# Feature attention into a PReLU MLP on one core: the last three token tiles on a permuted copy of x, other store shapes, fillers in the head, and a new order of all work

## The chip, the core and the metric

The kernel runs on one core of one Trainium2 chip. The core has TensorE (PE, matrix products, its weight loads shown apart as PEld), VectorE (DVE), ScalarE (ACT), GpSimd (POOL) and SyncE (SP, which here only issues transfers), each with its own queue worked through in order, and 16 DMA engines between the chip's memory (HBM) and the on-chip SBUF. PE writes into PSUM, eight banks of 128 partitions by 512 float32. The metric is the device time of one execution in microseconds (us), as the median of several runs; lower is better.

## The reference

An attention without softmax: queries and keys become 64 features each (the products of two 8-wide sketches), and every head's output is a ratio of two sums over these features. The heads' outputs, 4 x 1088 tokens of 4 x 32 = 128 columns, are the input x of an MLP with a hidden width of 2048 and a leaky relu whose slope `alpha` differs by column.

```python
def phi(x):                       # S1, S2: 8 x 32
    a = np.einsum('rd,bhsd->bhsr', S1, x)
    b = np.einsum('rd,bhsd->bhsr', S2, x)
    return np.einsum('bhsi,bhsj->bhsij', a, b).reshape(*x.shape[:-1], r * r)
q_p, k_p = (phi(q), phi(k))       # q, k, v: 4 batches, 4 heads, 1088, 32
kv = np.einsum('bhsf,bhsd->bhfd', k_p, v)
z = np.sum(k_p, axis=2)
num = np.einsum('bhsf,bhfd->bhsd', q_p, kv)
den = np.einsum('bhsf,bhf->bhs', q_p, z)[..., None] + 1e-06
x = (num / den).transpose(0, 2, 1, 3).reshape(4352, 128)
h = x @ w_in                      # 128 x 2048
g = np.maximum(h, 0.0) + alpha * np.minimum(h, 0.0)
out = g @ w_out                   # 2048 x 128
```

## The kernel before

**The MLP.** The leaky relu is split as alpha * h + (1 - alpha) * relu(h). The linear part is one 128 x 128 matrix W = w_in diag(alpha) w_out, made once (`Wmm`, copied by `W`). So the output is x W + relu(x w_in) w_a, with w_a = (1 - alpha) w_out. x lies in SBUF as `x_sb`, one column for each token and 128 partitions for the heads' columns. A batch has 34 groups of 32 tokens that came from 128-partition loads in which partition p holds tokens 34p to 34p + 33; so the columns are not in token order.

**The tiles.** `mlp` (L618) is called for ten tiles: tiles 0 to 6 have 512 tokens (two of each batch but the last), tile 7 ("the rest tile") takes the last 64 columns of all four batches, 256 tokens, and tiles 8 and 9 have 256 tokens each of the last batch. In a tile, `h` steps (L632) multiply x with 128 columns of w_in into a bank, `r` steps (L643 on ACT, L645 on DVE) apply relu and write bfloat16 into one of ten buffers `rh`, `o` steps (L653, L655) multiply with w_a and add up in the tile's output bank, and a `W` step adds x W. A name such as r8.12 is tile 8, hidden chunks from 12 on; in tiles 7 to 9 a step covers two chunks, with four 128-column matmuls in an `o` step (L653). Tiles 0 to 6 come out with output columns on partitions; DVE transposes them (`oT`, L683) and four stores go out per tile (L695). Tiles 7 to 9 take x or relu as the stationary operand and come out with tokens on partitions: two copies (`oT7.0`, `oT7.1`, L690) and a store of rows (L708, `store_rows`, two stores for tile 9, one on SP and one on ACT). For that, their relus write a permuted layout (L640), and their W step is eight matmuls of 32 columns of x each (L663).

**The attention.** For each batch, keys are transposed on DVE (`k1T0`), multiplied by the sketch (`k1f0`, L480), transposed back (`k1fT0`), multiplied elementwise (`k1p0`, mostly on POOL), summed (`zs10`, L504, and `z`/`zS`/`C`) and multiplied with v (`kv10`, L515, then `kvc`, `fin`, `kvR`). Queries run alike (`q1T0`, `q1f`, `q1t`, `q1rc`, `q1b`, `q1p0`, `q1p1`, `q1PT0`, `q1PT1`, `q1n` on PE at L547, and `q1x0`, `q1x1`, which write x). The first 512 queries of batch 0 take a shorter way: `qaT0` and `qaT1` (L563), `qaa0` to `qab1` (L571), `qac`, `qam`, the denominators `den0` and `den1` (L580) with `zcB`, the reciprocals `rc0` and `rc1` (L589), the numerators `num0` and `num1` (L594), and `xA0` and `xA1` (L596). The head is bound by these steps while k, q, v and the weights arrive.

**The order.** Nothing is scheduled at run time. A string `ORDER` (L22) names every step once, with its engine (p, a, d, g for POOL, s) and the numbers of the buffers it takes (PSUM banks and SBUF slots); `arrange` (L93) issues the steps in that order, and each engine has its steps in its queue in that order. A number behind the p is a count of filler matmuls issued ahead of the step (`dummy`, L274), products of constants whose result nobody reads; `warm` is 34 such units at the start.

Of the kernel before, what the change touches and what calls it, by code (L numbers as in the profile page):

```python
# [34 lines left out]
w_hi2:a r1.7:a:7 Wmm0:p:2 Wmm1:p kv10:p:6 r1.6:a:0 k2T0:d:0 q1rc:d:1 r1.5:a:8 r1.4:a:9 q1b:d k2f0:p:4 w_lo2:d Wmm2:p Wmm3:p h1.8:p:3 r1.2:a:3
h1.9:p:7 k3T0:d:1 k2fT0:d:0 kvc1:a:1 fin1:p W:d k3f0:p:4 zs20:p:2 r1.9:a:2 h1.10:p:7 r1.10:a:5 r1.3:d:4 W1:p:0 o1.0:p q1p0:g:0 q1PT0:d:1 o1.1:p
o1.2:p k3fT0:d:1 r1.8:a:6 h1.11:p:7 q1p1:g q1PT1:d o1.3:p o1.4:p o1.5:p h1.12:p:4 o1.6:p W0:p oT0:d:0 o1.7:p z12:a:0 k3p1:g:2 o1.8:p r1.12:a:1 zS2:p
C2:d kvR1:a q1n:p:3 q2T0:d:2 r1.11:a:3 q1x0:a q1x1:d h1.13:p:1 h1.14:p:2 r1.14:a:4 r1.13:a:9 o1.9:p h1.15:p:7 o1.10:p ld_v3_2:s st0.0:s st0.1:s
st0.2:s st0.3:s h2.0:p:3 h2.1:p:4 o1.11:p r2.0:a:8 o1.12:p r1.15:d:0 r2.1:d:7 h2.2:p:5 h2.3:p:6 r2.2:a:6 o1.13:p h2.4:p:2 h2.5:p:7 h2.6:p:1 r2.3:a:2
o1.14:p o1.15:p oT1:d:1 q2f:p:3 q2fT:d:0 r2.5:a:5 W2:p:7 o2.0:p o2.1:p o2.2:p o2.3:p h2.7:p:0 r2.7:d:3 r2.4:a:1 o2.4:p h2.8:p:2 k3p0:g h2.9:p:3  # L40
h2.10:p:4 h2.11:p:5 r2.9:d:9 r2.8:d:4 o2.5:p k2p1:g:1 r2.6:a:0 r2.11:a:8 h2.12:p:1 h2.13:p:6 h2.14:p:0 o2.6:p o2.7:p r2.10:d:7 r2.13:a:6 h2.15:p:3
h3.0:p:5 r2.14:d:2 h3.1:p:2 r2.12:a:1 r3.0:a:5 q2t:g:0 q2rc:d:0 r3.1:d:0 q2b:d q2p1:d:0 h3.2:p:6 h3.3:p:4 o2.8:p o2.9:p h3.4:p:1 h3.5:p:0 h3.6:p:5
r2.15:a:3 r3.4:a:4 o2.10:p o2.11:p o2.12:p r3.2:a:9 r3.6:a:7 h3.7:p:3 r3.7:a:8 h3.8:p:2 h3.9:p:1 o2.13:p ld_v2:s o2.14:p r3.5:a:1 ld_q3:s h3.10:p:6
o2.15:p oT2:d:2 r3.9:a:6 k2p0:g r3.3:a:2 W3:p:5 o3.0:p r3.10:a:3 zs30:p:3 z13:d:1 q2p0:g ld_v2_1:s ld_v2_2:s st1.0:s st1.1:s st1.2:s st1.3:s ld_v3:s
ld_v2_3:s st2.0:s st2.1:s st2.2:s st2.3:s r3.8:a:5 kv20:p:0 kvc2:a:0 o3.1:p h3.11:p:1 q2PT0:d:0 zS3:p C3:d fin2:p q2PT1:d kvR2:a h3.12:p:7 h3.13:p:4
h3.14:p:6 o3.2:p r3.11:a:0 o3.3:p r3.14:a:9 q3T0:d:0 o3.4:p o3.5:p r3.12:a:2 o3.6:p q2n:p:0 h3.15:p:6 q2x1:a r3.13:d:4 o3.7:p o3.8:p o3.9:p o3.10:p
# [12 lines left out]
st6.3:s h8.2:p:2 W7:p:3 r7.0:a:4 h8.4:p:1 r8.0:a:1 h8.6:p:7 o7.0:p h8.8:p:0 h8.10:p:5 r8.2:d:8 o7.2:p r8.6:a:3 o7.4:p o7.6:p h8.12:p:2 r7.10:a:4
# [53 lines left out]
def kernel(  # L113
# [39 lines left out]
    def ps(b):  # L153
        return PS[:, b.slot] if b.n == 1 else PS[:, b.slot:b.slot + b.n]
# [614 lines left out]
```

## Time and profile before

| | us |
|---|---|
| median of 3 runs | 109.92 (109.7 to 110.33) |
| the profiled execution, its own time | 110.14 |
| its span, from first to last instruction | 108.0 |
| PE busy / DVE busy / ACT busy / POOL busy | 96.0 / 80.6 / 64.9 / 46.0 |
| last matmul ends | 100.2 |
| mean granted TensorE clock | 0.959 |

The profile's page gives busy times, the span in 40 slices and the chain of work that ended last; answers of the trace give stretches (busy time of each engine, granted clock and DMA share between two moments), the timeline, waits, and the DMA issues with the time to landing. Some 2.1 us of an execution lie outside its span. PE's busy time counts pipelined matmuls from start to end, so that a row may be longer than the distance to the next one: 0.22 us from one 512-column product to the next, while one lasts 0.38.

### The profile page before, as it was taken

What the parts mean: (1) busy time and instruction counts of PE and PEld (TensorE: products, weight loads), DVE (VectorE), ACT (ScalarE), POOL (GpSimd) and SP (SyncE); (2) the same over time, 40 slices, a digit from 0 to 9 for tenths busy, and PEclk for the clock granted to TensorE, in tenths of its full rate; (3) what the DMA queues carried; (4) which work ended last, traced back from release to release, by engine and by line L of the source; (5) the groups of instructions that cost most, each with busy time, mean ns of one, the idle gap of its engine ahead of it and who ended that gap; (6) DMA issues with size and microseconds to landing.
All of it is one profiled execution on the core that took longest, in us unless ns stands there. A gap on an engine that the chain in (4) does not pass through costs nothing.

```text
span 108.0 us, 3355 instructions
## 1 busy us (share of the span) xinstructions
PE 96.0 (89%) x1402; PEld 54.3 (50%) x1402; DVE 80.6 (75%) x134; ACT 64.9 (60%) x139; POOL 46.0 (43%) x48
## 2 busy tenths in 40 slices
PE   7859888898999999999999999999999999999100
PEld 2414544686567545344464455444444466989000
DVE  4764799999899999589959847899598968545100
ACT  2302349999999265947997455685447666765000
POOL 4619306999998989709390004960000000000000
PEclk9985999999999999999999999999999999999955
DMA  3999999999200004784204100320310041510110
GB/s 84 324 250 336 367 273 294 289 297 225 71 3 9 6 0 72 217 230 77 72 14 71 19 6 0 60 37 6 67 30 0 0 76 27 97 48 6 52 40 8
DMA packets 21462, 11.24 MB, mean 104 GB/s; under 512 B 15416, under 2 KB 19912, under 8 KB 21448
## 3 DMA queue, kind: packets, MB, share of 16 engines
q1 hardware_dynamic: 21270, 10.95, 39.6%
q8 instruction: 11, 0.18, 0.7%
q10 hardware_dynamic: 178, 0.08, 0.3%
q14 instruction: 3, 0.02, 0.1%
HBM read 8.80 MB, written 2.23 MB: 102 GB/s over the span
## 4 chain that ended last, share of the span: by engine, by line
PE 77%; DVE 6%; DMA 5%; POOL 3%; ACT 1%; SPq 1%; issue 1%; DVEq 0%
PE ps L632 25%; PE ps L655 23%; PE ps L547 5%; PE ps L653 5%; DMA q<-in_q_dram 5%; PE ps L515 4%; PE ps L571 3%; POOL P__73 L187 2%; PE ps L439 2%; PE ps L480 2%; PE ps L379 2%; DVE rr__101 L589 2%; PE ps L398 1%; PE ps L504 1%; PE ps L580 1%; POOL w_a_bf L187 1%
## 5 line engine op out<-in xcount | busy, mean ns | idle before, releaser
L632 PE MATMUL ps<-x,w_in_bf 128*128 128x512 bf16 (+1 forms) x176 | 38.9, 331 | 0.5 <-DVE x L596 0.3
L632 PEld LDWEIGHTS <-w_in_bf 128*128 128x128 bf16 x176 | 16.5, 98 | 13.6 <-issue 2.0
L655 PEld LDWEIGHTS <-w_a_bf 128*128 128x128 bf16 x128 | 12.2, 98 | 11.5 <-POOL w_a_bf L187 0.6
L643 ACT ACTIVATE rh__87<-ps 128x512 bf16<-128x512 f32 x10 | 6.1, 605 | 4.9 <-PE ps L632 2.9
L643 ACT ACTIVATE rh__83<-ps 128x512 bf16<-128x512 f32 x12 | 7.4, 618 | 2.0 <-PE ps L632 2.0
L643 ACT ACTIVATE rh__91<-ps 128x512 bf16<-128x512 f32 (+1 forms) x12 | 7.1, 591 | 0.8 <-PE ps L655 0.8
L643 ACT ACTIVATE rh__90<-ps 128x512 bf16<-128x512 f32 x9 | 5.5, 615 | 3.3 <-PE ps L632 3.1
L643 ACT ACTIVATE rh__85<-ps 128x512 bf16<-128x512 f32 x10 | 6.2, 619 | 2.1 <-PE ps L632 2.1
L187 POOL TENSOR_TENSOR P__72<-Fk__70 128x1024 f32<-128x1024 f32 (+1 forms) x2 | 4.3, 2167 | 5.3 <-DVE Fk__70 L485 5.3
L643 ACT ACTIVATE rh__84<-ps 128x512 bf16<-128x512 f32 x8 | 4.9, 616 | 1.7 <-PE ps L632 1.7
L180 ACT CAST x<-ps 128x576 bf16<-128x576 f32 (+1 forms) x5 | 2.9, 597 | 4.8 <-PE ps L547 4.7
L645 DVE TENSOR_SCALAR rh__82<-ps 128x512 bf16<-128x512 f32 x7 | 4.8, 679 | 1.3 <-PE ps L632 1.2
L643 ACT ACTIVATE rh__88<-ps 128x512 bf16<-128x512 f32 x9 | 5.5, 609 | 0.3 <-PE ps L632 0.2
L187 POOL TENSOR_TENSOR P__71<-Fk__69 128x512 f32<-128x512 f32 (+1 forms) x4 | 4.1, 1062 | 3.0 <-DVE Wf L182 3.0
L187 POOL TENSOR_TENSOR t__77<-F__68 128x288 f32<-128x288 f32 x2 | 1.6, 784 | 8.7 <-DVE F__68 L442 8.7
L643 ACT ACTIVATE rh__82<-ps 128x512 bf16<-128x512 f32 x8 | 4.9, 608 | 0.3 <-PE ps L632 0.3
L643 ACT ACTIVATE rh__86<-ps 128x512 bf16<-128x512 f32 x8 | 4.9, 606 | 0.4 <-PE ps L632 0.2
L655 PE MATMUL ps<-rh__83,w_a_bf 128*128 128x512 bf16 (+1 forms) x15 | 4.9, 351 | 0.0
L571 PE MATMUL ps<-qTa,Sab 32*64 32x256 f32 x32 | 3.8, 585 | 1.3 <-DVE qTa L563 1.3
L187 POOL TENSOR_TENSOR P__71<-F__68 128x1152 f32<-128x1152 f32 x2 | 4.6, 2336 | 0.5 <-DVE F__68 L187 0.5
L645 DVE TENSOR_SCALAR rh__86<-ps 128x512 bf16<-128x512 f32 x7 | 4.7, 670 | 0.2 <-PE ps L632 0.2
L645 DVE TENSOR_SCALAR rh__89<-ps 128x512 bf16<-128x512 f32 x6 | 4.1, 683 | 0.7 <-PE ps L632 0.6
(201 smaller groups left out, 236.9 us busy)
## 6 DMA issues: line engine op xcount, KB each, us to landing
v<-in_v_dram SPq DMA_DIRECT2D x12, 144.0 KB, 5.0
k<-in_k_dram SPq DMA_DIRECT2D x3, 544.0 KB, 9.2
q<-in_q_dram SPq DMA_DIRECT2D x3, 544.0 KB, 7.6
w_in_f<-in_moe_w_in_dram SPq DMA_DIRECT2D x2, 512.0 KB, 7.5
w_out_f<-in_moe_w_out_dram SPq DMA_DIRECT2D x4, 256.0 KB, 8.3
out_dram<-oT__92 SPq DMA_DIRECT2D x9, 64.0 KB, 1.8
out_dram<-oT__93 SPq DMA_DIRECT2D x8, 64.0 KB, 1.9
out_dram<-oT__95 SPq DMA_DIRECT2D x8, 64.0 KB, 1.9
```

The costliest lines, as they stand in the source:

```text
L180: nc.scalar.copy(dst, src)
L187: (nc.vector if e == "dve" else nc.gpsimd).tensor_tensor(out=dst, in0=a, in1=b, op=what)
L379: nc.tensor.matmul(ps(bw)[:, :DM], winT[:, c], w_hl[:, c, y], start=c == y == 0, stop=c == NC - 1 and y == 1)
L439: nc.tensor.matmul(ps(bf)[32 * g:32 * g + 32, h, :n], Wf[32 * h:32 * h + 32, b], src[1]()[32 * h:32 * h + 32, g * n:(g + 1) * n], start=Tr ...
L515: nc.tensor.matmul(ps(bk)[32 * h:32 * h + 32, :R], v_sb[b][:, h, j], bview(sb(P), [[1, R]], (4 * j + h) * R), start=j == 0, stop=j == JG - ...
L547: nc.tensor.matmul(ps(bn)[32 * h:32 * h + 32, g, :n], kvR[b][32 * g:32 * g + 32, y, 32 * h:32 * h + 32], bview(sb(Q)[32 * g:32 * g + 32], ...
L571: nc.tensor.matmul(ps(bp)[64 * (h % 2):64 * (h % 2) + 64, h // 2, 256 * y:256 * y + 256], bview(Sab[32 * h:32 * h + 32, y], [[1, R]]), qTa ...
L632: nc.tensor.matmul(ps(b)[:, n * i:n * i + n], w_in_bf[:, c], x(), start=True, stop=True, skip_group_check=len(cs) > 1)
L643: nc.scalar.activation(dst, src, ACTF.Relu)
L645: nc.vector.tensor_scalar_max(dst, src, 0.0)
L653: nc.tensor.matmul(ps(bo)[:, j // JB, DM * (j % JB):DM * (j % JB) + DM], rhs(j), w, start=False, stop=end, skip_group_check=True)
L655: nc.tensor.matmul(ps(bo)[:, lo:lo + n], w, rhs, start=first and lo == 0, stop=end, skip_group_check=True)
```

## The change

- Tiles 7 to 9 read x from a new buffer `xp` (three pieces of 256 columns). A step `xp0`, `xp1` or `xp2` copies each tile's columns from `x_sb` in another order, in which four columns of one partition of the loads lie side by side. `xp0` and `xp1` run on DVE, `xp2` on POOL.
- With it the relus of these tiles read and write straight, their W step is two matmuls of 128 columns, and partition 4a + b of the output holds row b of group a. The store of a tile goes out as one transfer whose outermost index has 32 values, with 4 rows of 1 KB inside; tile 9's second store, on ACT, is gone.
- `alT` (the transposed alpha) comes at the start of PE's work, with two fillers ahead, and `qaa1` has three fillers ahead.
- The cost of one load (`rate` of qa) that the planner of the order used is another; it has no effect at run time.
- `ORDER` is new throughout: order, engines and buffers.

```diff
-ld_k0.0:s wz:g ident:g pads9:g ld_rows:a zero:d ld_rows_1:a ld_k0.1:s selP:d M8i:d ld_qa:s warm:p M4:d ld_v0:s M8b:d identb:g E8:d M64:d ld_v0_1:s
...
+ident:g M8b:d M4:d ld_rows:a ld_k0.0:s pads:g ld_rows_1:a ld_k0.1:s ld_alpha:a warm:p alT:p2:0 zero:d table:a alTc:a selP:g M2:d k0T0:d:0 k0T1:d
...
     def mlp(g, halves, store, wfirst, xw=None, final=False):
-        bo = Buf("ps", 2 if xw else 1)
-        J = halves[0][0] // 128
-        JB = J // 2
+        bo = Buf("ps", 1 if xw is None else 2)
...
-                def re(e, b=b, br=br, w=w, nu=len(cs)):
-                    src, dst = ps(b)[:, :w], sb(br)[:, :w]
-                    if xw:
-                        src, dst = (bview(t, ap) for t, ap in ((ps(b), [[32 * J, 4 * nu], [32, J], [1, 32]]),
-                                                               (sb(br), [[32, 4 * nu], [128 * nu, J], [1, 32]])))
+                def re(e, b=b, br=br, w=w):
                     if e == "act":
-                        nc.scalar.activation(dst, src, ACTF.Relu)
+                        nc.scalar.activation(sb(br)[:, :w], ps(b)[:, :w], ACTF.Relu)
...
         def put(e, c, rhs, lo, n, w, first, end):
-            if xw:
-                for j in range(J):
-                    nc.tensor.matmul(ps(bo)[:, j // JB, DM * (j % JB):DM * (j % JB) + DM], rhs(j), w, start=False, stop=end, skip_group_check=True)
+            if xw is not None:
+                for j in range(2):
+                    nc.tensor.matmul(ps(bo)[:, j, :DM], rhs[:, 128 * j:128 * j + 128], w, start=first, stop=end, skip_group_check=True)
...
         def wp(e):
-            if xw:
-                for j in range(J):
-                    for i in range(4):
-                        nc.tensor.matmul(ps(bo)[32 * i:32 * i + 32, j // JB, DM * (j % JB):DM * (j % JB) + DM], xw(J * i + j), W_bf,
-                                         start=j % JB == 0, stop=False, skip_group_check=True)
-                return
...
-    def store_rows(off, outer, parts=(("sp", 4),)):
-        def st(g, os, boT, rows_of, J):
-            lo = 0
-            for i, (en, k) in enumerate(parts):
-                op({en: 600}, lambda e, lo=lo, k=k: (nc.scalar if e == "act" else nc.sync).dma_start(
-                    bass.AP(tensor=out.tensor, offset=off + lo * outer, ap=[[outer, k], [NJ * DM, 32], [1, J * DM]]),
-                    rows_of()[32 * lo:32 * lo + 32 * k, :J * DM]), os, [boT], name=f"st{g}.{i}", nbytes=16384 * J * k, rate=300.)
-                lo += k
+    def store_rows(off, step):
+        def st(g, os, boT, rows_of):
+            op({"sp": 600}, lambda e: nc.sync.dma_start(bass.AP(tensor=out.tensor, offset=off, ap=[[NJ * DM, 32], [step, 4], [1, 2 * DM]]),
+                                                        rows_of()[:, :2 * DM]), os, [boT], name=f"st{g}.0", nbytes=131072, rate=300.)
         return st
+
+    def paired(t, off, step, needs):
+        o = op({"pool": 600, "dve": V(256, "sb"), "act": A(256, "sb")}, lambda e: copy(
+            e, bview(xp[:, t], [[128, 2], [4, 32], [1, 4]]), bview(x_sb, [[32, 2], [1, 32], [step, 4]], off)), needs, name=f"xp{t}", port=True)
+        return [(256, lambda: xp[:, t], [o])]
...
-    mlp(g + 3, [(256, cols(B - 1, 768, 256), xs[B - 1])], store_rows(row0 + 24 * DM, 2 * DM, (("sp", 2), ("act", 2))), True, tile_of(B - 1, 768), True)
+    mlp(g + 3, paired(2, col0 + 768, 64, xs[B - 1]), store_rows(row0 + 24 * DM, 2 * DM), True, 2, True)
```

Three places of the new order, word for word as the instructions stand in the engines' queues.

SP's last rows before: `oT__95` holds tile 6's output here, `oT__94`, `oT__93` and `oT__92` those of tiles 7, 8 and 9 (behind the buffer stands the shape of the transfer).

```order
L695 DMA out_dram<-oT__95 32x16x32 x4
L708 DMA out_dram<-oT__94 128x256
L708 DMA out_dram<-oT__93 4x32x256
L708 DMA out_dram<-oT__92 2x32x256
L764 UNCONDITIONAL_BRANCH
```

SP's last rows in the changed kernel, tile 6 and then tiles 7 to 9:

```order
L682 DMA out_dram<-oT__92 32x16x32 x4
L693 DMA out_dram<-oT__93 32x4x256
L693 DMA out_dram<-oT__95 32x4x256
L693 DMA out_dram<-oT__92 32x4x256
L749 UNCONDITIONAL_BRANCH
```

The outermost count of tiles 7, 8 and 9 was 128 (its two outer dimensions are one), 4, and 2 on SP with 2 on ACT; now it is 32 for all three, and ACT has no store.

ACT in tiles 7 to 9 before, from r8.14 to r9.2 (the `rh` names are the relus' output buffers, `oT2__94` is tile 7's output):

```order
L643 ACTIVATE rh7__89<-ps_63 128x8x2x32
L643 ACTIVATE rh9__91<-ps_63 128x8x2x32
L180 COPY oT2__94<-ps_63 128x128
L643 ACTIVATE rh2__84<-ps_63 128x8x2x32
L180 COPY oT2__94<-ps_63 128x128
L643 ACTIVATE rh6__88<-ps_63 128x8x2x32
```

ACT in the changed kernel, r8.6, r8.8, r8.4, r8.0, r8.12, r8.10 and r9.2:

```order
L637 ACTIVATE rh1__83<-ps_63 128x512
L637 ACTIVATE rh7__89<-ps_63 128x512
L637 ACTIVATE rh9__91<-ps_63 128x512
L637 ACTIVATE rh4__86<-ps_63 128x512
L637 ACTIVATE rh2__84<-ps_63 128x512
L637 ACTIVATE rh5__87<-ps_63 128x512
L637 ACTIVATE rh0__82<-ps_63 128x512
```

Tile 7's two output copies have moved from ACT to DVE, and seven relus stand one behind the other on ACT.

PE in the head before, from the first products of k on (`Fk__69` holds the sketched keys of batch 0, `qTa` the first 512 queries):

```order
L480 MATMUL ps<-T__64,Wk 32x288 x8
L571 MATMUL ps<-qTa,Sab 64x256 x4
L504 MATMUL ps<-Fk__69 32x32 x4
L571 MATMUL ps<-qTa,Sab 64x256 x8
L504 MATMUL ps<-Fk__69 32x32 x5
L571 MATMUL ps<-qTa,Sab 64x256 x4
```

PE in the changed kernel, from the last of the three fillers behind the products of k on:

```order
L276 LDWEIGHTS const-bfloat16-1.0
L276 MATMUL ps<-const-bfloat16-1.0 128x128
L571 MATMUL ps<-qTa,Sab 64x256 x8
L504 MATMUL ps<-Fk__69 32x32 x9
L571 MATMUL ps<-qTa,Sab 64x256 x8
L421 MATMUL ps<-zA,E_124 128x32
```

The z sums (L504) have come together between the two halves of the query products (L571), of which the second 256 queries now come first.

109 lines of the change are left out of this document (53 added, 56 removed).

## The prediction

> **What bounds the kernel now.** I read the page first (span, busy shares), then its chain that ended last by engine, and then the busy time by stretches (each row: from, to, length, then each engine's busy time, the granted clock, the DMA share and GB/s).
>
> ```profile
> span 108.0 us, 3355 instructions
> PE 96.0 (89%) x1402; PEld 54.3 (50%) x1402; DVE 80.6 (75%) x134; ACT 64.9 (60%) x139; POOL 46.0 (43%) x48
> PE 77%; DVE 6%; DMA 5%; POOL 3%; ACT 1%; SPq 1%; issue 1%; DVEq 0%
> core 0: us, PE busy (x) PEld busy (x) DVE busy (x) ACT busy (x) POOL busy (x), PEclk, DMA share, GB/s
> 3.65:7.07 3.42, 2.04 (x24) 0.91 (x22) 2.31 (x7) 0.00 (x0) 0.98 (x4) 1.00 1.05 272
> 7.07:10.48 3.41, 3.25 (x35) 1.32 (x35) 2.19 (x6) 0.58 (x1) 2.83 (x3) 0.50 1.00 313
> 13.90:30.00 16.10, 14.71 (x309) 9.85 (x308) 15.34 (x26) 14.78 (x40) 12.66 (x10) 1.00 0.90 235
> 30.00:100.20 70.20, 70.18 (x967) 39.38 (x965) 56.37 (x84) 46.62 (x93) 26.33 (x16) 1.00 0.23 48
> ```
>
> Three stages with three limits. From 30.0 to 100.2 PE is busy 70.18 of 70.20 us at full clock: no order of the same matmuls can make this stage shorter, only fewer matmuls can, and a worse order can make it longer. Before 30 PE idles and once runs at half clock (7.07 to 10.48); DVE, busy 15.34 of 16.10 us, sets the pace there. Behind 100.2 nothing computes, and yet 7.8 us of the span are left. From the timeline, the chain, SP's waits, the stretches and the DMA issues (last number: us from issue to landing):
>
> ```profile
> 100.16 0.29 DVE L182 COPY oT__92<-ps 128x128 f32<-128x128 f32 x1 [0.53 <-PE ps L653]
> 100.20 0.02 issue
> 100.54 0.54 SPq L708 DMA_DIRECT2D out_dram<-oT__92  x1
> 100.54 0.64 ACTq L708 DMA_DIRECT2D out_dram<-oT__92  x1
> SPq L764 <- DMA out_dram<-oT__92: 5.1, 2, 3.8
> 96.50:97.50 1.00, 1.00 (x19) 0.79 (x16) 0.08 (x1) 0.67 (x2) 0.00 (x0) 1.00 0.37 131
> 101.00:102.50 1.50, 0.00 (x0) 0.00 (x0) 0.00 (x0) 0.00 (x0) 0.00 (x0) 1.00 0.25 82
> 103.00:104.50 1.50, 0.00 (x0) 0.00 (x0) 0.00 (x0) 0.00 (x0) 0.00 (x0) 0.50 0.13 37
> out_dram<-oT__94 SPq DMA_DIRECT2D x1, 128.0 KB, 1.7
> out_dram<-oT__94 SPq DMA_DIRECT2D x4, 64.0 KB, 3.3
> ```
>
> SP issues the last store at 100.54, is done with that at 101.08, and then waits 5.1 us for the two halves of tile 9's output: 106.2. The remaining 1.8 us to 108.0 are the closing waits and the barrier. While those stores run, the DMA share is 0.25 (4 of 16 engines) and then 0.13 (2 of 16). The rest tile's store has the same 128 KB and landed in 1.7 us.
>
> **The tail: the store's shape.** SP's last rows stand in the section on the change. The outermost count goes from 128, 4 and 2 (twice, the other half on ACT) to 32 for all three. The shares above fit the outermost count: 128 spread wide (0.37 as a mean over a whole microsecond, though 128 KB were through), 4 took 4 engines, 2 took 2. With 32 I expect all 16, eight 1 KB rows each, as for tile 7. Then: last matmul to issue 0.34 us (100.54 - 100.20, the two copies are unchanged), issue to landing 1.7, closing 1.8: 3.84 in place of 7.8, so **-3.96 us**. Nothing is queued before it that could hide or delay it: tile 8's store is issued about 1.7 us earlier and is through by then. Bounds: no store in the trace lands under 1.7, so the gain is no larger; the slowest kind (3.3, above) would leave -2.4. I take 1.7, the row of equal size.
>
> The Trainium skill ("DMA: Bandwidth & Descriptors", the section on the anatomy of one DMA) speaks against a full gain: it gives each DMA a fixed part of about 2.0 us, mostly the write's receipt, which more engines do not divide, plus bytes over 436 GB/s (0.3 us here). By that the last store would take about 2.3 us, an estimate from that page, and the gain would be 3.4; the measured 1.7 us for 128 KB decides.
>
> **The tail: fewer W products.** In tiles 7 to 9 the product with W was eight 32-column matmuls and becomes two of 128 columns.
>
> ```profile
> 90.77 0.23 PE ps L663 x8
> 93.31 0.22 PE ps L653 x4
> 93.53 0.22 PE ps L632 x2
> ```
>
> Two 128-column matmuls are half of an o step of four: 0.11 for 0.23, three times: **-0.36 us**, on PE's full stage. The o steps keep their count. The relu reads and writes straight now, where it permuted in these three tiles; the two groups of 128x512 below hold both kinds, 605 ns on ACT and 684 ns on DVE, and a single one of tile 9 (0.61 at 97.81) stands at that mean, so nothing is to be gained.
>
> The permuted copies (`xp0`, `xp1` on DVE, `xp2` on POOL, 256 columns each) are new. The relus' rows, and the nearest ones for the copies:
>
> ```profile
> L643 ACT ACTIVATE rh__87<-ps 128x512 bf16<-128x512 f32 x10 | 6.1, 605 | 4.9 <-PE ps L632 2.9
> 97.81 0.61 ACT L643 ACTIVATE rh__82<-ps 128x512 bf16<-128x512 f32 x1
> L596 DVE TENSOR_TENSOR x<-ps,rr__100 128x256 bf16<-128x256 f32 x1 | 0.4, 386 | 0.0
> L645 DVE TENSOR_SCALAR rh__87<-ps 128x512 bf16<-128x512 f32 x3 | 2.1, 684 | 1.1 <-PE ps L653 1.1
> 1.52 0.33 POOL L295 CAST identb<-ident 128x128 bf16<-128x128 f32 x1
> 80.00:90.00 10.00, 10.00 (x57) 5.43 (x56) 7.98 (x14) 7.23 (x14) 0.00 (x0) 1.00 0.13 22
> ```
>
> 0.39 us on DVE (0.29, the 128-column copy, to 0.68), and 0.33 to 0.7 on POOL. DVE has 2 us free in these 10, and POOL is idle, so I cost them at 0; without that cover, 0.8 us of relu delay. W7 waits for `xp0`, and behind W7 the whole of tiles 7 to 9 is queued on PE; but `xp0` stands on DVE most of tile 6 ahead of W7. That cover is some 5 us.
>
> **The tail: ACT's order.** ACT's rows are shown with the change. Both copies of tile 7's output went to DVE, and ACT now has seven relus in a row, r8.6, r8.8, r8.4, r8.0, r8.12, r8.10 and r9.2. h9.6 needs bank 1, which r8.12 frees. Counting from h7.14: h8.6 ends at 1.8, and five relus of 0.6 end at 4.8. PE has by then h7.14, W7, eight o, W8 and eleven h, 20 x 0.217 + 2 x 0.11 = 4.6. So PE waits 0.2: **+0.2 us** (0, with ACT one step ahead, to 0.8, one relu late).
>
> **The middle.** Two rows, a load of v and a query product on POOL:
>
> ```profile
> v<-in_v_dram SPq DMA_DIRECT2D x12, 144.0 KB, 5.0
> L187 POOL TENSOR_TENSOR P__71<-F__68 128x1152 f32<-128x1152 f32 x2 | 4.6, 2336 | 0.5 <-DVE F__68 L187 0.5
> ```
>
> The loads that are moved stay covered: `v3_1` now stands on SP behind the stores of tile 2, which wait for DVE's `oT2`; its user kv30 comes two tiles later (a tile's 33 steps of 0.217 are 7 us), against 5.0 us for a v load to land. One of q2's products goes from DVE to POOL (2.3 us); POOL is busy 26 of 70 us. I take 0, with +1.5 as the bound (below).
>
> **The head.** PE's rows are shown with the change. The z sums (L504) come in one piece between the q products (L571). From the chain of before:
>
> ```profile
> 1.67 5.03 DMA q<-in_q_dram
> 7.22 1.13 PE ps L571 x8
> 8.35 0.27 PE ps L504 x8
> 8.62 1.91 PE ps L571 x16
> 10.53 0.24 PE ps L504 x10
> 10.78 0.59 PE ps L571 x8
> 12.97 1.08 PE ps L580 x8
> 18.13 1.66 DVE rr__101 L589
> 22.36 2.54 POOL P__73 L187 x2
> 24.89 1.01 POOL w_a_bf L187
> 25.95 0.61 PE ps L655 x4
> ```
>
> The q load lands at 6.70 in both, and the work behind it, 3.63 us of q products and 0.5 of z sums, is the same; the fillers fall into PE's idle time before it. In the new order the product that the first denominator needs is made second and not first; walking DVE and PE by these durations I reach the denominators (L580) at 13.1 for 12.97. Behind them DVE loses one small copy (alpha's) and gains another (z1's). So POOL's products start at about 22.5 for 22.36, and `w_a3` and PE's last wait behind them move alike: **+0.15 us**, within -1.2 (next part) and +0.7.
>
> **Sum**, against the profiled execution: -3.96 - 0.36 + 0.2 + 0.15 = -3.97, so a span near 104.0, and 110.14 - 3.97 = 106.17 (the 2.1 us of the execution that lie outside its span stay). The median shown (109.92) is 0.22 below that execution, within the runs' own spread of 0.6. In the median's frame: **106.0**.
>
> **The rivals.**
> - *The half clock goes.* The granted clock fell to 0.50 for 3.41 us behind a stretch in which PE was busy 2.04 of 3.42 us. The fillers and the earlier alpha product add about 0.4 us there. If that is enough, eight q products take 0.59 in place of 1.13, and the reciprocals come 0.5 to 1.2 us sooner: about 105.1. By the Trainium skill ("TensorE: Matmul & The Clock Gate", Part 1) the rate falls only behind an idle window; on that rule this stretch should not have been throttled, and fillers could change nothing, which leaves 106.0. The trace does not agree, as PE was 60% busy in it. 13%.
> - *Late ACT steps.* The thread kv30, kvc3, fin3, kvR3, q3n, q3x0, h6.0 is drawn tight: 5 PE steps (1.1 us) between q3n and h6.0, where 13 stood before, and every ACT step stands behind relus. Each one late by a relu costs 0.6; three of them 1.8: 107.8. For it: q3n is moved by a tile. Against: ACT is busy only 7.23 of 10 us there. 12%.
> - *The same, twice over and with the clock.* If PE stands still for over 1.4 us (40% of 3.42) at q3n and again at h6.0, each stretch is followed by 3.41 us of half clock: 2 x (1.4 + 1.7) = 6.2 us lost against 4 gained: 112.2, slower. It decides from two such stops on; ACT would have to be more than two relus behind both times. 4%.
> - *The store is not spread.* If the 32 still went to 4 engines, 128 KB at the 82 GB/s of the row with share 0.25 would take 1.6 us, some 1.2 more than spread wide: 107.2. The three shares speak against it. 5%.
>
> **How the numbers follow.** The forecast, 106.0, has 66%. The range takes in the early clock and the one-sided delays: 104.6 to 107.7. A measurement of this kernel can tell about 0.5% (0.55 us) from no change. Faster by more than that holds for all cases but the stopped clock and half of an unforeseen stall: 0.93; within 0.5%: 0.03; slower: 0.04.
>
> **What would show it.** The DMA share behind the last matmul near 16 engines for under a microsecond, and SP's last wait under 2 us; W steps of two matmuls; PE busy without a gap from 30 us to its end; the last matmul near 99.9 to 100.2; the clock row with its 0.5 at the same place. It is wrong if PE shows gaps behind ACT or DVE between 60 and 95 us, or if the last wait stays near 5 us.

## The result and the profile after

| | before | changed |
|---|---|---|
| device time, median (all runs) | 109.81 (109.48 to 110.33, 4) | 106.45 (105.98 to 108.12, 4) |
| profiled execution: time, span | 110.14, 108.0 | 108.12, 106.3 |
| last matmul ends | 100.2 | 102.0 |
| from there to the span's end | 7.8 | 4.2 |

The ratio of the times is 0.968 (95% interval 0.960 to 0.975; it leaves out runs that lie over 1.5% above the fastest of their kernel, as the profiled execution does): the changed kernel is faster by 3.4 us. Two later series of the same file, below, gave 0.969 (0.960 to 0.978) and 0.970 (0.966 to 0.975). But the profile does not show the way there that was forecast: the end of the matmuls came later, not earlier, and all the gain of this execution lies behind it.

The page of the changed kernel, its first lines and its chain by engine:

```profile
span 106.3 us, 3327 instructions
PE 98.4 (93%) x1388; PEld 56.2 (53%) x1388; DVE 80.3 (76%) x130; ACT 66.5 (63%) x138; POOL 49.6 (47%) x53
PE 69%; POOL 15%; DMA 5%; issue 3%; DVE 2%; SPq 1%; ACT 1%; POOLq 0%
```

PE has 14 matmuls fewer (1402 before) and yet more busy time: at half clock the same matmul takes longer. Its busy time by stretches (from, to, length, then each engine, granted clock, DMA share, GB/s) shows where:

```profile
3.65:7.07 3.42, 2.27 (x29) 1.14 (x27) 2.50 (x8) 0.50 (x3) 0.00 (x1) 1.00 1.04 266
7.07:10.48 3.41, 2.95 (x42) 1.69 (x46) 1.93 (x8) 0.76 (x2) 2.51 (x3) 0.51 1.01 302
10.48:13.90 3.42, 3.35 (x60) 2.13 (x54) 3.12 (x6) 1.03 (x4) 1.87 (x3) 0.50 1.06 364
13.90:17.40 3.50, 3.50 (x64) 1.85 (x62) 2.57 (x2) 0.87 (x3) 0.00 (x0) 0.51 1.12 333
40.00:102.00 62.00, 62.00 (x793) 34.33 (x777) 48.40 (x72) 42.62 (x83) 21.53 (x13) 1.00 0.21 40
```

Before, the half clock held for one stretch of 3.41 us. Here it held from 7.1 to 17.4 us, three such stretches, the last two with PE busy almost throughout. From 40 us to its end PE is busy without a gap. For the tail, the timeline of the last matmul, copy and store:

```profile
101.74 0.27 PE L647 MATMUL ps<-w_a_bf,rh__87 128*128 128x128 bf16 x2
102.05 0.29 DVE L182 COPY oT__92<-ps 128x128 f32<-128x128 f32 x1 [1.01 <-issue]
102.42 0.54 SPq L693 DMA_DIRECT2D out_dram<-oT__92  x1
```

SP's last wait (us in total, times, longest), and the stretches behind the last matmul:

```profile
SPq L749 <- DMA out_dram<-oT__92: 1.4, 1, 1.4
```

```profile
103.50:104.50 1.00, 0.00 (x0) 0.00 (x0) 0.00 (x0) 0.00 (x0) 0.00 (x0) 1.00 0.38 131
104.50:106.00 1.50, 0.00 (x0) 0.00 (x0) 0.00 (x0) 0.00 (x0) 0.00 (x0) 1.00 0.02 5
103.62:104.11 0.49, 0.00 (x0) 0.00 (x0) 0.00 (x0) 0.00 (x0) 0.00 (x0) 1.00 0.76 268
```

The stretches behind the last matmul before:

```profile
100.64:102.40 1.76, 0.00 (x0) 0.00 (x0) 0.00 (x0) 0.00 (x0) 0.00 (x0) 1.00 0.25 74
102.50:104.50 2.00, 0.00 (x0) 0.00 (x0) 0.00 (x0) 0.00 (x0) 0.00 (x0) 0.53 0.13 40
104.50:105.85 1.35, 0.00 (x0) 0.00 (x0) 0.00 (x0) 0.00 (x0) 0.00 (x0) 0.50 0.10 34
```

The DMA issues of tiles 7 and 9 (last number: us from issue to landing):

```profile
out_dram<-oT__93 SPq DMA_DIRECT2D x1, 128.0 KB, 2.2
out_dram<-oT__92 SPq DMA_DIRECT2D x1, 128.0 KB, 2.0
```

Tile 9's 128 KB go through in 0.49 us, at a DMA share of 0.76. Before, by the trace's DMA records, three transfers followed one another: the 128 packets of tile 8's store up to 102.4 (share 0.25), SP's 64 packets of tile 9 from there to 104.5, and ACT's 64, issued at 100.54, from 103.8 to 105.9. So tile 8's store was part of the long tail, and tile 9's two halves, each with an outermost count of 2, had no more than about two engines between them (share 0.13). SP's last wait is 1.4 us in place of 5.1. A store lands 2.0 to 2.2 us after its issue; the row of before on which the forecast rested had 1.7.

### The profile page after: what moved, and what is told of

It reads as the page before. It is cut to its first block, busy times and chain, and to the rows that moved or that the text cites. A ratio compares the mean times of both kernels' runs of the same rounds, so it can differ in the third digit from the quotient of the medians.

```text
span 106.3 us, 3327 instructions
## 1 busy us (share of the span) xinstructions
PE 98.4 (93%) x1388; PEld 56.2 (53%) x1388; DVE 80.3 (76%) x130; ACT 66.5 (63%) x138; POOL 49.6 (47%) x53
## 4 chain that ended last, share of the span: by engine, by line
PE 69%; POOL 15%; DMA 5%; issue 3%; DVE 2%; SPq 1%; ACT 1%; POOLq 0%
PE ps L630 23%; PE ps L649 21%; DMA q<-in_q_dram 5%; PE ps L647 4%; PE ps L547 4%; PE ps L515 4%; POOL P__72 L187 4%; POOL w_a_bf L187 4%; PE ps L571 4%; POOL P__73 L187 2%; POOL w_hl L187 2%; POOL w_in_f L187 2%; PE ps L580 2%; PE ps L379 2%; PE ps L439 1%
## 5 line engine op out<-in xcount | busy, mean ns | idle before, releaser
L630 PE MATMUL ps<-x,w_in_bf 128*128 128x512 bf16 (+1 forms) x128 | 31.7, 353 | 0.1
L637 ACT ACTIVATE rh__83<-ps 128x512 bf16<-128x512 f32 x12 | 7.3, 610 | 1.5 <-PE ps L630 1.4
L187 POOL TENSOR_TENSOR F__68<-F__68,rd__79 128x288 f32<-128x288 f32 x2 | 1.4, 680 | 13.2 <-DVE rd__79 L532 13.2
L637 ACT ACTIVATE rh__82<-ps 128x512 bf16<-128x512 f32 x10 | 6.1, 614 | 1.7 <-PE ps L630 1.7
L630 PE MATMUL ps<-xp,w_in_bf 128*128 128x256 bf16 x48 | 7.0, 273 | 0.0
L637 ACT ACTIVATE rh__84<-ps 128x512 bf16<-128x512 f32 x11 | 6.6, 599 | 0.6 <-PE ps L649 0.2
L639 DVE TENSOR_SCALAR rh__90<-ps 128x512 bf16<-128x512 f32 x7 | 4.8, 688 | 2.3 <-PE ps L630 2.2
L637 ACT ACTIVATE rh__86<-ps 128x512 bf16<-128x512 f32 x10 | 6.0, 603 | 0.8 <-PE ps L630 0.8
L637 ACT ACTIVATE rh__88<-ps 128x512 bf16<-128x512 f32 x9 | 5.4, 601 | 1.4 <-PE ps L630 1.4
L637 ACT ACTIVATE rh__91<-ps 128x512 bf16<-128x512 f32 x9 | 5.5, 607 | 1.2 <-PE ps L630 0.7
L637 ACT ACTIVATE rh__89<-ps 128x512 bf16<-128x512 f32 x8 | 4.8, 602 | 1.9 <-PE ps L630 1.5
L639 DVE TENSOR_SCALAR rh__85<-ps 128x512 bf16<-128x512 f32 x7 | 4.8, 679 | 1.1 <-PE ps L630 0.6
L637 ACT ACTIVATE rh__87<-ps 128x512 bf16<-128x512 f32 (+1 forms) x9 | 5.1, 572 | 0.6 <-PE ps L630 0.4
L637 ACT ACTIVATE rh__85<-ps 128x512 bf16<-128x512 f32 x7 | 4.2, 597 | 1.1 <-PE ps L630 1.1
L276 PE MATMUL ps<-const-bfloat16-1.0 128*128 128x512 bf16 (+1 forms) x15 | 3.9, 417 | 0.8 <-PEq L738 0.8
L187 POOL TENSOR_TENSOR w_in_f<-w_out_f,alphaT 128x512 f32<-128x512 f32 x2 | 2.1, 1040 | 5.4 <-ACT w_in_bf L180 5.4
```

Of the source, the lines that this page charges most:

```text
L187: (nc.vector if e == "dve" else nc.gpsimd).tensor_tensor(out=dst, in0=a, in1=b, op=what)
L276: nc.tensor.matmul(PS[:, 7, :m], ones(128), ones(m), start=True, stop=True, skip_group_check=True)
L630: nc.tensor.matmul(ps(b)[:, n * i:n * i + n], w_in_bf[:, c], x(), start=True, stop=True, skip_group_check=len(cs) > 1)
L637: nc.scalar.activation(sb(br)[:, :w], ps(b)[:, :w], ACTF.Relu)
L639: nc.vector.tensor_scalar_max(sb(br)[:, :w], ps(b)[:, :w], 0.0)
```

## The experiments

In the table, **clock** is what the trace's record of the granted clock shows in the head: the moment at which the clock rises to full (the record begins there; ahead of it the page prints 1.00 although PE runs at half), and whether it falls again. "Tail" runs from the end of the last matmul to the end of the span. One profiled execution each.

| kernel | clock rises, falls | last matmul | tail | span | times (median) |
|---|---|---|---|---|---|
| before | 3.7, at 7.1 for 3.4 | 100.18 | 7.79 | 108.0 | 109.48 to 110.33 (109.81) |
| changed | 3.7, at 7.1 for 10.2 | 102.02 | 4.24 | 106.3 | 105.98 to 108.12 (106.45) |
| e1 | 5.2, no | 100.09 | 3.70 | 103.8 | 105.42 to 107.05 (106.32) |
| e2 | 3.7, at 7.1 for 3.4 | 100.30 | 4.33 | 104.6 | 103.97 to 107.02 (104.36) |
| e3 (changed) | 4.0, no | 98.75 | 4.26 | 103.0 | 104.10 to 105.82 (104.99) |
| e4 | 4.6, no | 98.51 | 4.24 | 102.7 | 104.53 to 107.60 (105.79) |
| e5 | 4.2, no | 99.38 | 7.12 | 106.5 | 107.63 to 110.54 (108.58) |
| e6 | 9.7, no | 100.26 | 4.25 | 104.5 | 104.38 to 107.42 (105.53) |
| e7 | 9.5, no | 100.37 | 4.25 | 104.6 | 104.60 to 108.02 (106.07) |
| e8 | 3.5, no | 97.73 | 4.30 | 102.0 | 104.27 to 106.92 (105.59) |
| e9 | 3.4, no | 98.55 | 4.25 | 102.8 | 104.39 to 106.30 (104.95) |
| e10 | 5.3, no | 99.83 | 4.25 | 104.1 | 105.36 to 106.34 (105.71) |
| e11 | 4.4, no | 98.55 | 4.51 | 103.1 | 105.08 to 105.64 (105.42) |
| e12 (changed) | 5.4, no | 98.36 | 4.25 | 102.6 | 104.39 to 107.32 (105.18) |

The kernel before, run beside them, had medians of 109.66 (e1 to e4, 107.50 to 112.86), 109.19 (e5 to e8, 107.53 to 110.92) and 108.37 (e9 to e12, 107.80 to 111.02).

### e1: only the stores of tiles 8 and 9, in the kernel before

```diff
-store_rows(row0 + 16 * DM, 2 * DM)
+store_rows(row0 + 16 * DM, 2 * DM, (("sp", 1), ("act", 1), ("sp", 1), ("act", 1)))
-store_rows(row0 + 24 * DM, 2 * DM, (("sp", 2), ("act", 2)))
+store_rows(row0 + 24 * DM, 2 * DM, (("sp", 1), ("act", 1), ("sp", 1), ("act", 1)))
```

(In `ORDER` the further stores of each tile stand behind its first one, two on SP and two on ACT.)

> The kernel before with nothing changed but the stores of tiles 8 and 9: four transfers of 32 rows each (outermost count 32), two issued by SP and two by ACT, in place of one of 4 x 32 and two of 2 x 32. If the outermost count sets how many DMA engines work, the last wait of SP falls from 5.1 us to about 2, and the second issue on each queue costs about 0.6: 2.5 to 3.5 us faster than before (106.3 to 107.3), with the DMA share behind the last matmul above 0.3. If the landing time of the last store is a fixed cost, or the engines are set by something else: no change (109.3 to 110.3).

Each of the four transfers of a tile has 32 rows in its outermost index. The tail is 3.70 us against 7.79, so 4.09 less; the 32 KB land in 1.5 to 1.7 us. Here the stores are also cut into four and spread over two queues, which the change does not do; what this run has in common with the changed kernel and with e2 (tails 4.24 and 4.33, one transfer for each tile) is the outermost count of 32. Together they show the shape of the transfers as the cause of the long tail. But the ratio of the times is only 0.981 (0.970 to 0.992), and the last matmul ended as late as in the profile of before although the clock had not fallen. The timeline of this run, ACT's queue and PE's:

```profile
97.87 0.85 ACTq L708 DMA_DIRECT2D out_dram<-oT__93  x2
98.77 0.60 ACT L643 ACTIVATE rh__82<-ps 128x512 bf16<-128x512 f32 x1 [2.31 <-DVE rh__90 L645]
99.42 0.40 PE L653 MATMUL ps<-w_a_bf,rh__82 128*128 128x128 bf16 x4 [1.15 <-ACT rh__82 L643]
```

Tile 8's two transfers on ACT are issued only when DVE has written the output, and take 0.85 us to issue; one of tile 9's last relus stands behind them, and PE waits 1.15 us for it. The changed kernel, whose stores are all on SP, has no such wait.

### e2: the edits in the order of before

```diff
-r6.0:d:9 o5.8:p
+r6.0:d:9 xp0:d xp1:d xp2:g o5.8:p
-oT9.1:a st9.0:s st9.1:a
+oT9.1:a st9.0:s
```

> The changed kernel's code with the order of the kernel before (three steps xp0, xp1, xp2 put in behind r6.0, st9.1 taken out; buffers and engines as before). If the new order is worth nothing, as forecast (+0.35 us): 105.5 to 106.5, the same as the changed kernel within 0.5. If the new order carries part of the gain: slower than the changed kernel by that part, 107 or more. If the new order costs time in the head: faster, 105 or less.

Ratio 0.964 (0.957 to 0.971), against 0.969 (0.960 to 0.978) for the changed kernel in the same series: the new order brings nothing that can be measured. The one cost of leaving the old order as it was is the two copies on DVE, ahead of a relu that PE waits for (PE's waits from 75 us on, then DVE's timeline):

```profile
PE ps L630 <- DVE rh__82 L639: 0.4, 1, 0.4
```

```profile
81.55 0.67 DVE L182 COPY xp<-x 128x256 bf16<-128x256 bf16 x2
82.14 0.68 DVE L639 TENSOR_SCALAR rh__82<-ps 128x512 bf16<-128x512 f32 x1
```

The profile has the same clock in the head as that of before and can be laid beside it: the span fell by 3.34, the tail by 3.46, and the last matmul moved by +0.12 (the product W gave 0.36, the copies took 0.42).

### e3 and e12: the changed kernel again

> The changed kernel itself again, beside the others on the same chip and for a second trace. 105.9 to 106.5; span about 104.1 where the half clock lasts 3.4 us in the head, about 106.3 where it lasts 10.2 us. Last wait of SP 1.4 us as in its first profile.

> The changed kernel unchanged, as the reference for these runs on the same chip. Expected by both theories: 104.1 to 106, median near 105, with some runs of 106 to 108 where the clock rises late or falls again in the head.

In both profiles the clock does not fall in the head, and the last matmul ends 3.3 and 3.7 us earlier than in the first profile of the same file. The stretch ahead of the possible fall, of e3:

```profile
3.65:7.07 3.42, 3.10 (x42) 1.79 (x43) 3.42 (x12) 0.50 (x3) 0.25 (x2) 1.00 1.07 285
7.07:10.48 3.41, 2.91 (x84) 1.73 (x76) 2.93 (x8) 1.58 (x5) 3.41 (x4) 1.00 0.98 337
```

The file is the same; what differs in the records is when the loads landed and how the stretches of the clock lie. In the first profile PE waited 1.0 us for alpha, and the first products with k began at 5.92; here they began at 5.23, the query products at 6.38 in place of 7.53, and PE was busy 3.10 us of 3.42 instead of 2.27. The sixteen runs of the changed kernel in three series lie from 104.10 to 108.12.

### e4: the changed kernel without its fillers

```diff
-alT:p2:0
+alT:p:0
-qaa1:p3:5
+qaa1:p:5
```

> The changed kernel without the five filler matmuls ahead of alT and qaa1. If five fillers are too few to move the clock (forecast): the same as the changed kernel within 0.5 us, with the half clock from about 7.2 us on. If they are what keeps the half clock short: more executions with 10 us of half clock, 1 to 2 us slower.

The clock did not fall here either (PE busy 2.62 of 3.42 us in the stretch). Ratio 0.970 (0.961 to 0.979): the fillers as the change has them neither bring nor cost what can be measured.

### e5 and e6: more fillers

e5, in the kernel before:

```diff
-qaa0:p:4
+qaa0:p16:4
```

e6, in the changed kernel:

```diff
-qaa1:p3:5
+qaa1:p12:5
```

> The kernel before, with 16 filler units (about 0.85 us of bf16 products on constants) ahead of qaa0, in PE's wait for the first q load; the results are unchanged. Theory (the half clock follows too little PE work in the stretch before it): PE's busy time from 3.65 to 7.07 rises from 2.04 to 2.8 or more, no row of the clock shows 0.50, the head is 1.45 us earlier (the difference measured between before and the spread stores, whose clock stayed whole), the last matmul ends near 98.8, and the time is near 108.5 with a spread under 1.5 us. Rival (the clock is dropped by something other than PE's own work, and differs from run to run anyway): half of the runs still show a granted clock under 0.98 and times of 109.5 and more.

> The changed kernel with 12 filler units in place of 3 ahead of qaa1 (0.5 us more of filler products in the wait for q); the results are unchanged. Theory (the spread of the changed kernel's times, 104.1 to 108.1, is the clock in the head): no 0.50 row, span 102.5 to 103.3, times within 104.2 to 105.2, never over 106. Against the kernel before with fillers the gain is then that of tail, W and middle alone: -3.55 - 0.36 + 0.7 = -3.2. Rival (the spread is that of loads): times still from 104 to 108 at a clock of 1.0.

Half right. Neither profile shows a fall. But e5's ratio to the kernel before is 0.999 (0.995 to 1.004) and its times still spread over 2.9 us. e6's ratio is 0.965 (0.958 to 0.971), and its three slowest times (106.20, 106.29 and 107.42) all come with a granted clock of 1.00: the theory that the fall explains the spread fell. The timeline of PE in e6 shows another delay, at a granted clock that the page gives as 1.00:

```profile
5.39 0.77 PE L324 MATMUL ps<-rows,selP 16*128 16x128 f32 x2
6.09 1.21 PE L480 MATMUL ps<-T__64,Wk 64*32 64x288 f32 x16
8.63 1.61 PE L571 MATMUL ps<-qTa,Sab 32*64 32x256 f32 x16
10.47 0.88 PE L571 MATMUL ps<-qTa,Sab 32*64 32x256 f32 x12
```

In e3, e4 and e9 the two products of L324 take 0.46, the sixteen of L480 0.72, the sixteen of L571 1.09; here all take longer up to 9.7 us, and behind it twelve of L571 take 0.88, the full rate. Until about 9.7 us PE ran at half clock, not because the clock had fallen but because it had not yet risen. It stands at half at the start of every profile (products of 512 columns among the fillers begin 0.43 us apart ahead of the rise and 0.22 behind it), and the rise came at 3.4 to 5.4 us in twelve profiles and at 9.5 and 9.7 in two (e7 and this). The falls last 3.41 us or three times that, so the clock seems to be set once in a stretch of that length; how these stretches lie when the kernel starts is then a matter of chance.

### e7: v1_1 issued with its siblings

```diff
-ld_v1_2:s xA0:d
+ld_v1_2:s ld_v1_1:s xA0:d
...
-qbrc:d:0 ld_v1_1:s zS1:p
+qbrc:d:0 zS1:p
```

(and 12 fillers ahead of `qaa1`, as in e6.)

> The changed kernel with the 12 filler units, and with v1_1 issued on SP right behind v1_2, ahead of k2 and q2, where the new order has it behind both. Theory (kv10 waits for v1_1, the last of the four loads that it needs): PE's gap inside L515 near 32 us (0.74 and 1.09 in two profiles) goes, PE is busy over 9.8 of 10 us from 30 to 40, and the time is 0.5 to 0.9 under that of the changed kernel with fillers alone. Rival (the gap is a wait for POOL's product k1p0, or for DVE): the gap stays and so does the time, within 0.2.

A miss. PE's gap in the middle of kv10 stayed, though the load now went out ahead of k2 and q2, and the median is 106.07 for e6's 105.53 (ratio to the kernel before 0.972, 0.964 to 0.980). Timeline of PE in this run, and of the one with the gap in the changed kernel (e3):

```profile
33.24 0.30 PE L515 MATMUL ps<-P__72,v 128*32 128x64 f32 x3
34.15 1.20 PE L515 MATMUL ps<-P__72,v 128*32 128x64 f32 x69 [0.61 <-issue]
```

```profile
31.49 0.30 PE L515 MATMUL ps<-P__72,v 128*32 128x64 f32 x3
32.53 1.20 PE L515 MATMUL ps<-P__72,v 128*32 128x64 f32 x69 [0.74 <-issue]
```

PE stops behind the third of 72 matmuls that all have the same needs, and waits for nothing that the profile names. The trace's DMA records show transfers that the kernel does not issue, on the page of the changed kernel as follows:

```profile
q8 instruction: 11, 0.18, 0.8%
```

0.18 MB over PE's 2776 instructions (1388 of each kind) is 65 bytes each. In five profiles PE stood still at kv10 (e3, e4, e5, e7, e10; 0.6 to 1.1 us), and it went on 2.72 to 2.84 us after one of these 16 KB transfers had begun (e7: 31.42 and 34.15; in e10 the gap stands ahead of the first matmul shown, and the profile puts it down to an ACT step). In the others the transfer had begun 3.2 us or more before kv10. The place of the stop says more. The stretches from the span's start to the inside of the gap give the number of matmuls (PE) and weight loads (PEld) begun by then, here for e3, e4, e7 and e10:

```profile
0.00:31.80 31.80, 28.61 (x473) 16.44 (x474) 27.43 (x51) 21.82 (x51) 23.90 (x38) 1.00 0.96 268
0.00:31.30 31.30, 27.89 (x473) 16.38 (x474) 26.72 (x51) 21.50 (x51) 24.04 (x38) 1.00 0.98 268
0.00:33.60 33.60, 31.15 (x473) 17.09 (x474) 27.07 (x51) 21.84 (x51) 23.96 (x38) 1.00 0.94 254
0.00:33.00 33.00, 29.78 (x474) 16.86 (x474) 27.44 (x51) 21.78 (x51) 23.88 (x38) 1.00 0.95 259
```

The count is the same to within one, but the place in kv10 is not: behind the third matmul in e3 and e7, behind the eighth in e4, which has no fillers, and ahead of the first in e10, which has more of them. A wait for v1_1 or for k1p0 would not move with the fillers. So the gap is, by all that can be seen, PE's wait for its own instructions (no run here moved these transfers at will), and not a cost of the change: e5 has the old order.

### e8 and e11: the old order with fillers, and the copies on POOL

Both, against e2:

```diff
-qaa0:p:4
+qaa0:p16:4
-xp0:d xp1:d xp2:g
+xp0:g xp1:g xp2:g
```

e11 besides:

```diff
-rowsT:p:0
+rowsT:p14:0
-store_rows(row0 + 24 * DM, 2 * DM)
+store_rows(row0 + 24 * DM, 2 * DM, (("sp", 16), ("act", 16)))
```

(In e11 `st9.1:a` stands at the end of the order again, as before.)

> The edits of the change in the order of before, as in the run with the old order, with 16 filler units ahead of qaa0 and all three permuted copies on POOL, which is idle there (three of 0.62 us), in place of two on DVE. Theory (the old order lost nothing but the half clock in some runs, and 0.42 us to the two DVE copies ahead of r6.3): PE busy 15.0 of 15 us from 80 to 95, no 0.50 row, span near 102.0, times 103.5 to 104.2, so faster than the changed kernel. Rival (the new order is worth something by itself): slower than the changed kernel with fillers, over 104.7.

> The edits in the order of before with all three permuted copies on POOL and 16 filler units ahead of qaa0 (as in the earlier run), and besides 14 filler units ahead of rowsT, and the last tile's store in two halves of 64 KB (16 in the outer index), one on SP and one on ACT. Theory: the clock rises by 6.2 us in every run and the last landing takes 1.7 in place of 2.0 to 2.2, so all runs lie from 103.5 to 104.6, median near 104.0, below the changed kernel. Rival (a landing does not depend on the size here, and the clock's rise not on the warm-up): 104 to 107, as the earlier run.

With the copies on POOL PE has no gap from 80 to 95 us (15.00 of 15.00, 14.58 in e2), and e8's profile has the shortest span of all, 102.0. Its other runs reach 106.92, though. In e11 the longer warm-up holds all runs within 0.56 us of each other, but they lie at 105.08 and above, for the first products with k begin at 5.98 in place of 5.15. The halved last store did not land sooner (DMA issues of e11):

```profile
out_dram<-oT__92 ACTq DMA_DIRECT2D x1, 64.0 KB, 2.2
```

Ratios: 0.964 (0.957 to 0.971) and 0.975 (0.972 to 0.978). Neither beats the changed kernel by more than the intervals.

### e9: five loads later

```diff
-qbPT0:d:0 ld_v2_2:s h0.10b:p:5 winT1:p:0 ld_v2:s h0.12b:p:1
+qbPT0:d:0 h0.10b:p:5 winT1:p:0 h0.12b:p:1
...
-o1.2:p ld_v2_3:s h1.12:p:4
+o1.2:p h1.12:p:4
...
-ld_v3:s ld_v3_2:s st0.0:s st0.1:s st0.2:s st0.3:s
+st0.0:s st0.1:s st0.2:s st0.3:s ld_v2_2:s ld_v2:s ld_v2_3:s ld_v3:s ld_v3_2:s
```

> The changed kernel with five of its later loads (v2_2, v2, v2_3, v3, v3_2: 0.72 MB) put on SP behind tile 0's stores, where the order of before had most of them. Theory (PE's gap inside kv10 is a fetch of PE's own instructions, 16 KB on a queue that stands behind the loads: in four runs with the gap it ended 2.65 to 2.85 us after such a fetch had begun, and in the runs without it the fetch had begun 3.2 us or more before kv10): with fewer loads in front the fetch starts by 28 us, the gap goes, PE is busy over 9.8 of 10 us from 30 to 40, and the time is 0.5 to 0.9 under the changed kernel's at the same clock in the head. Rival (kv10 waits for data): the gap stays.

The transfer of instructions began at 26.9, kv10 ran in one piece, and PE was busy 9.73 of 10 us from 30 to 40. But so it was in e12, beside it and unchanged (27.4; 9.72), with the DMA engines full of loads from 25 to 30. The ratio is 0.968 (0.963 to 0.973), for e12's 0.970. The run does not tell the theories apart; what decides when these 16 KB are fetched stays open.

### e10: a longer warm-up

```diff
-alT:p2:0
+alT:p18:0
```

> The changed kernel with 18 filler units in place of 2 between the warm-up block and alT; the results are unchanged. Theory (PE's clock starts at half and rises at the end of a 3.41-us stretch that was nearly full; with the few fillers it rose at 3.5 to 5.2 us in eight profiles and at 9.5 to 9.7 in two, as the stretches happened to lie): PE is now busy without a break to 5.2 us or later, so the clock rises by 6.2 us in every run; the times of 106 and over go, all runs lie from 104.2 to 105.6, with a median near 104.9. Rival (the late rise has another cause): some runs of 106 to 108 stay.

The spread is 0.98 us (2.93 for the unchanged kernel beside it, e12), as the theory of the rise says, as far as six runs can show it; no run of 106.5 or more is left, though three lie above the 105.6 that was expected. The ratio is 0.978 (0.974 to 0.982). But the fastest run is 0.97 slower than the unchanged kernel's fastest, and the median of 105.71 not below 105.18: PE's warm-up now ends at 5.96 and the first products with k start at 6.46. Timeline of PE:

```profile
0.77 5.19 PE L276 MATMUL ps<-const-bfloat16-1.0 128*128 128x512 bf16 x16 [0.77 <-PEq L738]
6.46 0.72 PE L480 MATMUL ps<-T__64,Wk 64*32 64x288 f32 x16
```

A filler that pins the clock costs here about what the late rise costs on average (mean of the six runs 105.77, of e12's 105.59).

## Why the prediction was right, point by point

The time came out at 106.45, for 106.0 in a range of 104.6 to 107.7. The mechanism was right, one size was off, and one term that was given as a number is not a number. That the time came so close is in part luck: which clock the four runs met in the head was chance, and in two later series the same file's medians were 104.99 and 105.18.

- **The store's shape, -3.96.** The mechanism is shown: with 32 in the outermost index the tail shrinks by 4.09 in e1 and by 3.46 in e2; in the change it is 7.79 to 4.24, **-3.55**. The rival of a store that is not spread falls with the share of 0.76. The term was mis-sized in one step, "issue to landing 1.7". The row of equal size that was taken has 128 in its outermost index, and landed in 1.7 again in e1 and e5. The new shape, 32 by 4 rows, lands in 2.0 to 2.2 at the same place in the work (tile 7) and at the end. By the Trainium skill ("DMA: Bandwidth & Descriptors", the anatomy of one DMA) the gain was estimated at 3.4, with 2.3 us for such a store, which is nearer to 3.55 than 3.96 is. But that section is on transfers issued from GpSimd, where SP issues these, and the 2.0 measured at the end lies as far from 2.3 as from 1.7. What else lies in the tail was right: 0.34 to 0.4 us to the issue, 1.8 behind the landing. The tail of before is itself no constant: it was 7.12 in e5.
- **Two W matmuls for eight, -0.36.** Six matmuls in place of 24, as forecast: the next step starts 0.12 us behind each step of two.
- **The permuted copies, 0.** 0.37 us each on DVE and 0.62 on POOL, and PE without a gap around them. e2 shows that the cover is a matter of place: both copies in front of one relu cost 0.42.
- **ACT's seven relus, +0.2.** Did not come. PE is busy without a gap from 40 us to its end, here and in e12 (55.00 us of 55.00 from 40 to 95); between 30 and 40 us it is not (9.71 us of 10). The rival of late ACT steps falls with it, as does its double with the clock at q3n and h6.0.
- **The middle, 0.** Up to 1.1 us of standing still at kv10, with the likely cause above: it comes in the old order too (e5), and is absent from half of the profiles of the new one.
- **The head, +0.15.** This is the step that failed, as a statement on any one run: the clock row was to show "its 0.5 at the same place", and in the change's first profile it showed 0.5 for 10.2 us in place of 3.4, so that the last matmul ended at 102.0, outside the 99.9 to 100.2 that was named. Where the clock agrees, the order does give next to nothing: the first denominators start at 11.37 in e5 and 11.43 in e12. But the clock does not agree from run to run. Between two executions of the same file (the first profile and e12) the last matmul moves by 3.7 us, as much as the whole gain. The rival "the half clock goes" named 105.1 and was met by e3 and e12 (medians 104.99 and 105.18), yet not for the reason given: without fillers (e4) the clock stayed whole as well, and it stayed whole in e1, which has the old order.

With like clocks the account closes. From before to e2 (both with one fall): tail -3.46, W -0.36, copies +0.42, rest +0.06, sum -3.34. From e5 to e12 (both without): tail -2.87, W -0.36, kv10's gap -0.60, rest -0.06, sum -3.89. The change's gain is the tail and W. The second pair differs in the order and in the fillers too, and 0.06 is what is left for both; as the clock rose 1.2 us later in e12 than in e5, costs may offset each other in it.

## What to carry to other kernels

Look behind the last matmul before anything else: here a DMA share of 0.25 and 0.13 there was the mark of outermost counts of 4 and 2, and a layout that made them 32 was worth about 3.5 us, where a new order of all work brought nothing that could be measured. A store issued just ahead of the last one belongs to the same account. Price such a store by the landing of a transfer of the same shape, not of the same size. And before one gives a term of a few tenths to a kernel's head, compare several profiles of the same file: where the clock rises or falls there, the runs differ by more than the edit.

## What the runs showed of the hardware

- **The start of the clock.** PE runs at half clock from its first matmul to a rise at 3.4 to 5.4 us in twelve of fourteen profiles, and at 9.5 to 9.7 us in two; the page's clock row shows none of that. The Trainium skill ("TensorE: Matmul & The Clock Gate", Part 1) says that the windows run free of the kernel's start, which these moments agree with. That a busy window of some 3.4 us brings the rise agrees less: in the first profile of the change PE was busy 3.35 of 3.42 us from 10.48 to 13.90, and the clock rose at 17.4 only; in e7 PE was busy all 3.41 us from 2.65 to 6.06, and the clock rose at 9.5. Its table gives an idle window as what brings the clock back to half (it does not say that nothing else can); here the clock fell behind stretches in which PE was busy 2.04 to 2.27 us of 3.42 (before, e2 and the first profile of the change), and stayed whole where the same stretch had 2.42 and more. But that is no threshold of PE's busy time: at the end of the work the clock stayed whole behind stretches with less, such as these of e11, e8 and e4 (counted back from the next fall in steps of 3.41 us).

```profile
96.54:99.96 3.42, 2.01 (x34) 1.82 (x32) 1.68 (x5) 0.93 (x3) 0.00 (x0) 1.00 0.14 43
95.65:99.06 3.41, 2.08 (x35) 1.87 (x32) 1.71 (x5) 1.00 (x3) 0.00 (x0) 1.00 0.13 43
96.71:100.12 3.41, 1.80 (x33) 1.62 (x30) 1.12 (x3) 0.70 (x3) 0.00 (x0) 1.00 0.15 46
```

In each the record shows the fall 3.4 us later, behind a stretch with PE idle. The matmuls there are bfloat16 of 128 rows, those in the head in part float32 of 16 to 64; what the hardware counts as busy was not tried and stays open.

- **A store's landing.** 128 KB as 128 rows of 1 KB landed in 1.7 us in e1 and e5, as 32 by 4 rows in 2.0 to 2.2, 64 KB as 16 by 4 rows in 2.2, 32 KB as 32 rows in 1.5 to 1.7. Bytes do not order these; why the nested shape is slower stays open.
- **PE's instructions.** In five profiles PE stood still for 0.6 to 1.1 us at one place of its own instruction stream (473 or 474 matmuls in the four of the new order), until 2.72 to 2.84 us after a 16 KB instruction transfer had begun; in four of the five the profile shows this as idle time that ended by "issue".
